# A gated recurrence followed by a soft mixture of experts: the filler transposes of the identity, which the planner puts where TensorE is free in the first chunks, are left out

## The chip, the cores and the metric

The kernel runs on one core of a Trainium2 chip. The metric is device time in microseconds (us) for one execution; lower is better. The core has five engines that this text speaks of: TensorE (PE in the profile, with its weight loads as PEld), VectorE (DVE), ScalarE (ACT), GpSimd (POOL), and SyncE (SP), whose queue issues the DMAs. TensorE runs at one of two clock levels, 1.2 and 2.4 GHz; the profile calls the granted share of the full level PEclk (0.50 and 1.00).

## What is computed

The input is a sequence of 4 x 5056 = 20224 tokens with 256 channels. A gated linear recurrence runs along each sequence, and its result, all tokens in one list, goes through a soft mixture of 8 experts with 4 slots each. Cut to what matters:

```python
a_base = sigmoid(a_param)                       # one number per channel
log_a = 8.0 * sigmoid(r_gate) * log(clip(a_base))
a_t = exp(log_a)
x_gated = sqrt(max(1 - a_t * a_t, 1e-6)) * sigmoid(i_gate) * x
for t in range(S):
    h = a_t[:, t] * h + x_gated[:, t]           # y[:, t] = h
x = y.reshape(B * S, D)                         # 20224 x 256
logits = x @ phi                                # 20224 x 32
d = softmax of logits over the tokens;  c = softmax of logits over the slots
slot_input = d.T @ x                            # 32 x 256
slot_out = relu(slot_input[e] @ w1[e]) @ w2[e]  # for each of 8 experts
out = c @ slot_out
```

## The kernel before

Tokens are taken in quads of 512 (number q), and quads in units p: unit 0 is quad 0 alone, then come units of two quads. Units are grouped in chunks of two, because ScalarE's functions live in different tables and each chunk goes through them once (tanh and exp, sigmoid, square root).

The work on one quad, with the names that the tasks have in the program:

- SP loads r_gate, i_gate and x of the quad (line 553; the first r_gate in two halves, lines 550 and 551) into seven buffers `st` and sixteen buffers `b`.
- TR (line 610): TensorE transposes the 512 x 256 block of r_gate, 8 transposes of 128 x 128, into a PSUM buffer of two banks, of which there are three, `pair_92`, `pair_93` and `pair_94`. At most two of them may be held by TR at a time.
- SR (line 621): ScalarE takes tanh of that block. EX (line 685) turns it into a_t, SQ (line 672, mostly GpSimd) squares it, RT (line 702) takes the square root.
- SI (lines 634 and 636): ScalarE's sigmoid or tanh of i_gate. P1 and U (lines 647 and 656): GpSimd multiplies it by x.
- TU (line 721): TensorE transposes that product into a `pair`, for one half of the channels of one unit: 8 transposes, or 16 where two terms are added.
- ST and SC (lines 738 and 755): VectorE multiplies by the root and runs the scan. SC of one unit continues from SC of the unit before.
- TY (line 779): TensorE transposes the scan's result back, 4 transposes for half a quad, into a single PSUM bank (`one_87` or `one_88`) or a `pair`. YC (lines 793 and 795) copies it to SBUF.

Groups of four quads then feed the logits (line 835), a running maximum (line 848) and the weighted sums over the tokens (line 909). After the last scan come the merge, the experts and the output (lines 1094 to 1390).

What sets the order: no engine chooses at run time. A planner (class `Planner`) plays the work through once, with estimated durations, and writes for each engine one fixed sequence of tasks. ScalarE's sequence of table functions is fixed ahead of that. Where TensorE is free in the plan, no task is ready for it, and the planned time is between `warm_from` (4.0) and `warm_to`, the planner puts in a filler task:

```python
elif e == "PE" and self.warm is not None and (self.warm_from <= now < self.warm_to or self.warm_late(self)):   # 279
    t = self.filler(now)
# filler (307): takes a single bank if more than one is free, else a pair if more than one is free
def e_warm(b):                                                                                                 # 1033
    for _ in range(2):
        nc.tensor.transpose(
            out=t(b)[:, 0, :P] if b.tag == "pair" else t(b)[:, :P], in_=ident, identity=ident)
planner.warm, planner.warm_from, planner.warm_to = e_warm, 4.0, WARMT                                          # 1038
```

A filler task is two transposes of the identity (line 1035). It holds a PSUM buffer from the same lists as the other tasks, nothing reads its result, and it has no input but the constant identity. `warm_late` is never true here, as `LATE` is False.

Of the kernel before, what the change touches and what calls it, by code (L numbers as in the profile page):

```python
# [39 lines left out]
YPM = 2  # L40
XPM = 0
YPQ = 0
WARMT = 60.0
QL = 99
TUP = 15
ACP = -4
# [327 lines left out]
def kernel(  # L374
# [662 lines left out]

    planner.warm, planner.warm_from, planner.warm_to = e_warm, 4.0, WARMT
    planner.pair_max = {"rp": RPM, "up": UPM, "yp": YPM, **dict.fromkeys(("lp", "ep", "ac", "cp"), XPM)}
# [392 lines left out]
```

## Time and profile before

| | |
|---|---|
| median of 3 runs | 305.94 us (305.58 to 306.07) |
| the profiled execution | 304.62 us |
| its span, first to last instruction | 302.8 us |
| its mean granted TensorE clock | 0.995 |
| instructions in the profile | 5814 |
| TensorE busy | 256.7 us, 85% |
| VectorE busy | 251.1 us, 83% |
| ScalarE busy | 250.1 us, 83% |
| GpSimd busy | 207.3 us, 68% |
| DMA | 100.03 MB, mean 330 GB/s |

How to read it: the profile is of one execution, and its 304.62 us hold the span of 302.8 us and 1.8 us around it; the median of the runs is 1.3 us above it. Busy shares are means over the whole span. They differ between the recurrence (to about 210 us), the merge and the experts (to about 245 us) and the output.

### The profile page before, as it was taken

Reading aid. Unit: us, or ns where it says so; the run is one execution under the profiler, and the core shown is the slowest. Engines: PE = TensorE matmul, PEld = TensorE weight load, DVE = VectorE, ACT = ScalarE, POOL = GpSimd, SP = SyncE. Lnnn points to the kernel's source line nnn. Section 1 sums busy time; section 2 is a strip of 40 time slices with the busy share of each in tenths; the row PEclk is TensorE's granted clock in tenths of the full one; section 3 lists DMA queues with packets and bytes.
Section 4 is the critical chain, followed back from the end, with each engine's and each line's share of the span. In section 5 each row is a group of like instructions: output and inputs, shape, how many; then the busy total and the mean of one; then the engine's idle time right before and its main releaser. Section 6 shows DMA issues by size and latency. Waiting matters only on the chain.

```text
span 302.8 us, 5814 instructions
## 1 busy us (share of the span) xinstructions
PE 256.7 (85%) x2181; PEld 191.9 (63%) x2181; DVE 251.1 (83%) x313; ACT 250.1 (83%) x273; POOL 207.3 (68%) x154
## 2 busy tenths in 40 slices
PE   6988759888779989889888988869999999999980
PEld 5977656765555756657566565465545588888760
DVE  0048769999999999899999999989968178999861
ACT  6899999999999999999999999999320058879540
POOL 4383996979969999999997996996216303456200
PEclk9999999999999999999999999999999999999998
DMA  6999899896995978939979889579999419999997
GB/s 249 416 411 409 302 349 333 309 374 260 375 415 206 386 285 295 358 125 360 414 238 374 336 280 411 190 286 393 393 387 388 160 67 391 405 392 407 385 406 288
DMA packets 30433, 100.03 MB, mean 330 GB/s; under 512 B 3395, under 2 KB 3397, under 8 KB 30405
## 3 DMA queue, kind: packets, MB, share of 16 engines
q1 hardware_dynamic: 30400, 99.66, 86.4%
q8 instruction: 17, 0.28, 0.4%
q14 instruction: 12, 0.09, 0.1%
q10 hardware_dynamic: 4, 0.00, 0.0%
HBM read 78.94 MB, written 20.71 MB: 329 GB/s over the span
## 4 chain that ended last, share of the span: by engine, by line
ACT 52%; PE 25%; DVE 9%; issue 7%; DMA 4%; POOL 0%; SPq 0%; DVEq 0%; ACTq 0%
ACT b L702 10%; ACT b L621 10%; ACT b L685 9%; PE bank L1363 8%; ACT st L634 6%; ACT L702 4%; DVE b L755 4%; ACT st L636 3%; ACT L621 3%; ACT L634 3%; PE one L1363 2%; PE bank L1206 2%; DVE pair L738 2%; DMA st<-in_r_gate_dram 2%; PE bank L1340 2%
## 5 line engine op out<-in xcount | busy, mean ns | idle before, releaser
L672 POOL TENSOR_TENSOR b<-b 128x1024 f32<-128x1024 f32 (+1 forms) x40 | 72.0, 1834 | 25.8 <-ACT b L685 23.3
L656 POOL TENSOR_TENSOR b<-st,b 128x1024 f32<-128x1024 f32 (+1 forms) x33 | 76.3, 2339 | 0.2
L738 DVE SCALAR_TENSOR_TENSOR pair<-b,pair 128x1024 f32<-128x1024 f32 (+2 forms) x42 | 48.1, 1155 | 8.9 <-PE pair L721 5.3
L721 PE MATMUL pair<-ident,b 128*128 128x128 f32 x316 | 43.8, 277 | 10.7 <-ACT b L621 5.8
L755 DVE TENSOR_TENSOR_SCAN b<-b,pair 128x1024 f32<-128x1024 f32 (+6 forms) x28 | 52.2, 1883 | 0.2
L610 PE MATMUL pair<-ident,st 128*128 128x128 f32 x316 | 42.6, 281 | 11.5 <-ACT b L621 5.4
L721 PEld LDWEIGHTS pair<-ident,b 128*128 128x128 f32 x316 | 34.5, 141 | 23.6 <-ACT b L621 7.7
L610 PEld LDWEIGHTS pair<-ident,st 128*128 128x128 f32 x316 | 35.0, 143 | 20.6 <-ACT b L621 10.2
L685 ACT ACTIVATE b<-b,ca 128x2048 f32<-128x2048 f32 (+3 forms) x24 | 42.5, 1796 | 0.2
L621 ACT ACTIVATE b<-pair 128x1024 f32<-128x1024 f32 (+1 forms) x40 | 39.9, 1005 | 2.8 <-PE pair L610 2.5
L755 DVE TENSOR_TENSOR_SCAN b<-b,b,pair 128x1024 f32<-128x1024 f32 (+2 forms) x20 | 40.9, 2047 | 0.3
L1363 PE MATMUL bank<-bd,hT 128*128 128x512 f32 x122 | 33.2, 401 | 1.8 <-ACT hT L1351 0.8
L779 PE MATMUL one<-ident,b 128*128 128x128 f32 x224 | 33.0, 278 | 0.6 <-DVE b L755 0.6
L795 DVE COPY yn<-one 128x512 f32<-128x512 f32 x47 | 30.8, 683 | 2.7 <-PE one L779 2.5
L702 ACT ACTIVATE b<-b 128x2048 f32<-128x2048 f32 (+2 forms) x18 | 31.7, 1791 | 0.1
L779 PEld LDWEIGHTS one<-ident,b 128*128 128x128 f32 x224 | 24.9, 141 | 5.6 <-DVE yn L795 2.3
L1306 POOL TENSOR_TENSOR b<-b,rs_all 128x512 f32<-128x512 f32 (+2 forms) x11 | 10.7, 975 | 24.2 <-DVE rs_all L1298 23.2
L1363 PEld LDWEIGHTS bank<-bd,hT 128*128 128x128 f32 x122 | 22.0, 188 | 6.7 <-ACT hT L1351 1.3
L634 ACT ACTIVATE st<-st 128x1024 f32<-128x1024 f32 x26 | 25.9, 1048 | 0.1
L835 PE MATMUL one<-b,phi_sb 128*32 128x512 f32 (+1 forms) x164 | 24.2, 585 | 1.2 <-ACT eS L889 0.7
L1375 ACT COPY st<-bank 128x512 f32<-128x512 f32 x32 | 18.0, 596 | 6.5 <-PE bank L1363 3.8
L1377 DVE COPY st<-bank 128x512 f32<-128x512 f32 x26 | 17.3, 680 | 4.3 <-DMA out_dram<-st 2.9
(143 smaller groups left out, 430.8 us busy)
## 6 DMA issues: line engine op xcount, KB each, us to landing
st<-in_i_gate_dram SPq DMA_DIRECT2D x39, 512.0 KB, 6.2
b<-in_x_dram SPq DMA_DIRECT2D x39, 512.0 KB, 7.0
st<-in_r_gate_dram SPq DMA_DIRECT2D x38, 512.0 KB, 7.3
out_dram<-st SPq DMA_DIRECT2D x35, 512.0 KB, 5.2
b<-in_moe_w_dram SPq DMA_DIRECT2D x26, 512.0 KB, 9.1
st<-in_moe_w_dram SPq DMA_DIRECT2D x6, 512.0 KB, 5.0
out_dram<-st SPq DMA_DIRECT2D x5, 256.0 KB, 2.9
out_dram<-b SPq DMA_DIRECT2D x2, 512.0 KB, 4.4
```

The source lines that it names most:

```text
L610: nc.tensor.transpose(out=o[:, m, :], in_=raw("r", q)[:, m * D + h * P : m * D + (h + 1) * P], identity=ident,)
L621: nc.scalar.activation(dst, t(rp)[:, :, :c], AF.Tanh, scale=0.5)
L634: nc.scalar.activation(v, v, AF.Sigmoid)
L656: eng.tensor_tensor(out=o, in0=a, in1=b, op=ALU.mult)
L672: eng.tensor_tensor(out=t(Nb[p])[:, h, :c], in0=v, in1=v, op=ALU.mult)
L685: nc.scalar.activation(v, v, AF.Exp, scale=ca[:, h : h + 1], bias=ca[:, h : h + 1])
L702: nc.scalar.activation(v, v, AF.Sqrt, bias=quarter if f != 1.0 else f, scale=-f)
L721: nc.tensor.matmul(o[:, m, :], raw(nm, q)[:, m * D + h * P : m * D + (h + 1) * P], ident, is_transpose=True, start=(nm == nms[0] and m == ...
L738: nc.vector.scalar_tensor_tensor(v, t(Nb[p])[:, h, :c], 0.5e-3 if gate_of(quads(p)[0]) == "E" else 1e-3, v, op0=ALU.max, op1=ALU.mult)
L755: nc.vector.tensor_tensor_scan(dst, dst, flat()[:, s0:s1], init, op0=ALU.mult, op1=ALU.add)
L779: nc.tensor.transpose(out=flat()[:, b * D + h * P : b * D + (h + 1) * P], in_=t(A[p])[:, h, o : o + P], identity=ident,)
L1363: nc.tensor.matmul(t(op), t(hT)[:, b * P // 2 : (b + 2) * P // 2], T["bd"][part].rearrange("p i d -> p (i d)"), start=(part == 0), stop=(p ...
```

## The change

One constant is set to zero:

```diff
-WARMT = 60.0
+WARMT = 0.0
```

With `warm_to` at 0.0 the condition on line 279 never holds, and the planner puts in no filler. TensorE's sequence loses the 56 filler tasks, 112 of its 2181 matmuls, and as many weight loads. The other tasks keep their order on ScalarE, VectorE, GpSimd and SP. What else differs is which of the like PSUM buffers a task gets, and one swap on TensorE.

The first place is TensorE's sequence at the start. `st_61`, `st_62` and `st_63` hold r_gate of quads 0, 1 and 2, `st_65` that of quad 3. Before:

```order
L937 MATMUL one_87<-ident,ap_sb 128x2
L610 MATMUL pair_92<-ident,st_61 128x128 x8
L1035 MATMUL one_88<-ident 128x128 x2
L1035 MATMUL pair_93<-ident 128x128 x2
L1035 MATMUL one_87<-ident 128x128 x2
L610 MATMUL pair_94<-ident,st_62 128x128 x8
L1035 MATMUL one_88<-ident 128x128 x2
L1035 MATMUL pair_93<-ident 128x128 x2
L1035 MATMUL one_87<-ident 128x128 x2
L1035 MATMUL pair_92<-ident 128x128 x2
L610 MATMUL pair_93<-ident,st_63 128x128 x8
```

The same place in the changed kernel:

```order
L937 MATMUL one_87<-ident,ap_sb 128x2
L610 MATMUL pair_92<-ident,st_61 128x128 x8
L610 MATMUL pair_93<-ident,st_62 128x128 x8
L610 MATMUL pair_94<-ident,st_63 128x128 x8
L610 MATMUL pair_92<-ident,st_65 128x128 x8
```

The TRs of quads 0 to 3 now follow each other, and the three pairs go round among them.

The second place is TensorE's sequence where the first back transposes (line 779, TY, of `b_68`) stand; `st_66`, `st_61` and `st_62` hold r_gate of the next quads. Before:

```order
L610 MATMUL pair_94<-ident,st_62 128x128 x8
L779 MATMUL one_88<-ident,b_68 128x128 x4
L779 MATMUL one_87<-ident,b_68 128x128 x4
L1035 MATMUL pair_93<-ident 128x128 x2
L1035 MATMUL pair_94<-ident 128x128 x2
L1035 MATMUL pair_93<-ident 128x128 x2
L1035 MATMUL pair_94<-ident 128x128 x2
L1035 MATMUL pair_93<-ident 128x128 x2
L1035 MATMUL pair_94<-ident 128x128 x2
L779 MATMUL one_88<-ident,b_68 128x128 x4
L610 MATMUL pair_93<-ident,st_66 128x128 x8
L779 MATMUL one_87<-ident,b_68 128x128 x4
```

The same place in the changed kernel:

```order
L610 MATMUL pair_94<-ident,st_62 128x128 x8
L779 MATMUL one_88<-ident,b_68 128x128 x4
L779 MATMUL one_87<-ident,b_68 128x128 x4
L779 MATMUL one_88<-ident,b_68 128x128 x4
L779 MATMUL pair_92<-ident,b_68 128x128 x4
L610 MATMUL pair_94<-ident,st_66 128x128 x8
L610 MATMUL pair_93<-ident,st_61 128x128 x8
L779 MATMUL one_87<-ident,b_68 128x128 x4
```

Six fillers are gone, and the fourth TY, now into `pair_92`, stands ahead of the TR of `st_66` where it stood behind it.

The third place is TensorE's sequence around the TUs of the third unit (`b_72`). Before, with eight fillers between its two halves:

```order
L779 MATMUL one_87<-ident,b_68 128x128 x4
L721 MATMUL pair_93<-ident,b_72 128x128 x8
L1035 MATMUL one_88<-ident 128x128 x2
L1035 MATMUL one_87<-ident 128x128 x2
L1035 MATMUL one_88<-ident 128x128 x2
L1035 MATMUL one_87<-ident 128x128 x2
L1035 MATMUL one_88<-ident 128x128 x2
L1035 MATMUL one_87<-ident 128x128 x2
L1035 MATMUL one_88<-ident 128x128 x2
L1035 MATMUL one_87<-ident 128x128 x2
L721 MATMUL pair_92<-ident,b_72 128x128 x8
```

The same place in the changed kernel:

```order
L779 MATMUL one_88<-ident,b_68 128x128 x4
L721 MATMUL pair_94<-ident,b_72 128x128 x8
L721 MATMUL pair_93<-ident,b_72 128x128 x8
L721 MATMUL pair_94<-ident,st_65 128x128 x4
L721 MATMUL pair_94<-ident,b_72 128x128 x4
```

The two TUs of the unit now stand next to each other. From here on both kernels have the same sequence on every engine, and the PSUM buffers of one are those of the other under exchanged numbers.

## Rows read from the trace of the kernel before

**Rows 1.** The page: its head, the busy time of each engine, and the chain of work that ended last, by engine.

```profile
span 302.8 us, 5814 instructions
PE 256.7 (85%) x2181; PEld 191.9 (63%) x2181; DVE 251.1 (83%) x313; ACT 250.1 (83%) x273; POOL 207.3 (68%) x154
ACT 52%; PE 25%; DVE 9%; issue 7%; DMA 4%; POOL 0%; SPq 0%; DVEq 0%; ACTq 0%
```

**Rows 2.** Busy time by stage: from and to, length, then busy us of PE, PEld, DVE, ACT and POOL (with their instructions), granted clock, DMA share, GB/s.

```profile
10.00:45.00 35.00, 27.25 (x234) 25.10 (x233) 20.76 (x18) 34.79 (x30) 26.69 (x13) 1.00 0.97 374
45.00:95.00 50.00, 41.91 (x358) 30.93 (x357) 48.30 (x49) 49.77 (x42) 42.35 (x24) 1.00 0.86 324
95.00:195.00 100.00, 86.30 (x769) 61.28 (x767) 97.91 (x99) 99.56 (x88) 94.23 (x52) 1.00 0.84 312
```

**Rows 3.** ScalarE in order of time: start, us from start to end, operation, count, and in brackets the idle time before it and what ended it.

```profile
5.44 1.02 ACT L621 ACTIVATE b<-pair 128x1024 f32<-128x1024 f32 x1 [1.26 <-PE pair L610]
...
7.46 1.03 ACT L621 ACTIVATE b<-pair 128x1024 f32<-128x1024 f32 x1
9.76 1.03 ACT L621 ACTIVATE b<-pair 128x1024 f32<-128x1024 f32 x1 [1.28 <-PE pair L610]
10.82 2.38 ACT L685 ACTIVATE b<-b,ca 128x1024 f32<-128x1024 f32 x2
...
15.70 1.92 ACT L621 ACTIVATE b<-pair 128x1024 f32<-128x1024 f32 x2
...
34.32 2.01 ACT L634 ACTIVATE st<-st 128x1024 f32<-128x1024 f32 x2
36.23 1.01 ACT L621 ACTIVATE b<-pair 128x1024 f32<-128x1024 f32 x1
...
43.68 1.94 ACT L621 ACTIVATE b<-pair 128x1024 f32<-128x1024 f32 x2
```

**Rows 4.** The fillers: all matmuls of line 1035, by the buffer that they write.

```profile
L1035 PE MATMUL one<-ident 128*128 128x128 f32 x72 | 11.7, 279 | 0.0
L1035 PE MATMUL pair<-ident 128*128 128x128 f32 x40 | 7.3, 283 | 1.8 <-ACT b L621 1.5 <-DVE b L755 0.3
```

**Rows 5.** TensorE in order of time from 3 to 17 us, matmuls and some of the weight loads (PEld) of the fillers.

```profile
3.22 2.18 PE L610 MATMUL pair<-ident,st 128*128 128x128 f32 x8 [0.79 <-DMA st<-in_r_gate_dram]
4.98 0.44 PEld L1035 LDWEIGHTS one<-ident 128*128 128x128 f32 x2
5.41 0.44 PEld L1035 LDWEIGHTS pair<-ident 128*128 128x128 f32 x2
6.38 1.04 PE L610 MATMUL pair<-ident,st 128*128 128x128 f32 x8
7.15 0.25 PEld L1035 LDWEIGHTS one<-ident 128*128 128x128 f32 x2
7.37 0.25 PEld L1035 LDWEIGHTS pair<-ident 128*128 128x128 f32 x2
8.63 1.09 PE L610 MATMUL pair<-ident,st 128*128 128x128 f32 x8 [0.34 <-DMA st<-in_r_gate_dram]
11.53 1.04 PE L610 MATMUL pair<-ident,st 128*128 128x128 f32 x8
```

**Rows 6.** The loads of r_gate of quads 1 and 2 on line 553, issued at 1.64 and 2.07 us: the issues in 2.05 to 2.5 us, and the time from issue to landing (shortest, median, longest of the two).

```profile
L553 SPq DMA_DIRECT2D st<-in_r_gate_dram x2: 424/428/432, 1.6 to 2.1; - x2
DMA to landing us min/median/max: 4.5/5.5/6.5
```

**Rows 7.** TensorE in order of time from 28 to 36 us.

```profile
28.83 1.04 PE L779 MATMUL one<-ident,b 128*128 128x128 f32 x8
30.14 0.44 PE L1035 MATMUL pair<-ident 128*128 128x128 f32 x2 [0.27 <-DVE b L755]
32.11 1.31 PE L1035 MATMUL pair<-ident 128*128 128x128 f32 x10 [1.53 <-ACT b L621]
33.26 0.27 PE L779 MATMUL one<-ident,b 128*128 128x128 f32 x1
34.10 0.55 PE L779 MATMUL one<-ident,b 128*128 128x128 f32 x3 [0.58 <-DVE b L755]
34.49 1.04 PE L610 MATMUL pair<-ident,st 128*128 128x128 f32 x8
```

**Rows 8.** TensorE in order of time from 40 to 46 us, and then rows of VectorE in order of time between 45 and 61 us.

```profile
40.44 0.66 PE L721 MATMUL pair<-ident,b 128*128 128x128 f32 x4 [1.39 <-POOL b L656]
40.94 1.91 PE L1035 MATMUL one<-ident 128*128 128x128 f32 x16
44.75 1.09 PE L721 MATMUL pair<-ident,b 128*128 128x128 f32 x8 [1.91 <-ACT b L621]
...
45.98 1.23 DVE L738 SCALAR_TENSOR_TENSOR pair<-b,pair 128x1024 f32<-128x1024 f32 x1 [1.16 <-PE pair L721]
59.25 1.29 DVE L795 COPY yn<-one 128x512 f32<-128x512 f32 x2 [0.39 <-PE one L779]
```

**Rows 9.** TensorE around its longest gap between two tasks, and its last matmuls.

```profile
196.10 0.60 PE L779 MATMUL one<-ident,b 128*128 128x128 f32 x4
198.87 1.09 PE L779 MATMUL pair<-ident,b 128*128 128x128 f32 x8 [2.17 <-ACT yn L793]
294.22 1.66 PE L1363 MATMUL bank<-bd,hT 128*128 128x512 f32 x6 [0.65 <-DVE hT L1353]
```

**Rows 10.** Busy time by stretch (columns as in rows 2), for the gap and for the end of the span: the granted clock is the third number from the end.

```profile
196.00:199.00 3.00, 0.83 (x8) 0.59 (x7) 2.80 (x2) 2.99 (x4) 3.00 (x2) 1.00 0.80 284
300.00:302.80 2.80, 0.00 (x0) 0.00 (x0) 0.00 (x0) 0.00 (x0) 0.00 (x0) 0.50 0.29 109
```

## The prediction

> **What bounds the kernel now.** I read the page first [rows 1]. TensorE has the largest busy share (85%), but in the chain of work that ended last ScalarE holds 52% and TensorE 25%. Means over the span say little about a change that ends at some 43 us, so the next view is the busy time by stage [rows 2]. From 10 to 195 us ScalarE works for 34.79 + 49.77 + 99.56 = 184.12 of 185 us: it is idle for 0.88 us in all. TensorE, in the stretch with the fillers, is busy for 27.25 of 35 us. So until 195 us the time is set by ScalarE's queue, which runs in a fixed order: what delays one of its instructions delays the rest one for one, as only 0.88 us of idle time can take it up; what makes another engine faster can return those 0.88 us at most.
>
> The third view is ScalarE's own order of time [rows 3]. It waits for TensorE twice, 1.26 us before the SR at 5.44 and 1.28 us before that at 9.76. Both wait for TRs that waited for DMA: the loads of quads 1 and 2 were issued at 1.64 and 2.07 and took 4.5 and 6.5 us, landing at 6.14 and 8.57 [rows 6], and the TR of quad 2 starts at 8.63 [rows 5]. No filler stands in that wait. The places to look at are therefore those at which a TR or a TU ends just before ScalarE or VectorE needs it, and the question there is how fast TensorE runs.
>
> **The fillers themselves.** The change takes away 72 + 40 = 112 matmuls with 11.7 + 7.3 = 19.0 us of busy time [rows 4]. TensorE's busy time should fall by about that, to some 238 us. None of it is on the path by its duration. Fillers that stand ahead of a TR cost that TR something (at 11.53, for instance), but the SR that reads it comes at 15.70 [rows 3, 5], 3.1 us after the TR's end. At 32.11 five fillers wait for ScalarE and stand ahead of the third TY; that TY begins at 33.26, its first transpose runs, and the other three wait until 34.10 for VectorE's scan, whose result they read [rows 7]. Without the fillers they wait for the same scan. So the removal by itself returns 0.0 us; the bounds are 0.0 and -0.88 us (the idle time above), and I take 0.0, since ScalarE's idle time shows no wait for TensorE after 9.76. On SP, VectorE and GpSimd nothing is moved; SP waits for TRs to free `st` buffers, and earlier TRs only let it issue earlier.
>
> **The swap.** The fourth TY now stands ahead of the TR of `st_66`, whose SR is at 36.23. Before, three transposes start at 34.10 and the TR's eight run from 34.49 to 35.53 [rows 7], 0.70 us ahead of the SR [rows 3]. Now 3 + 4 + 8 = 15 transposes lie between the scan's release at 34.10 and the TR's end. At the full clock the weight loads of fillers come two in 0.22 us (7.15 to 7.37), 0.11 us each [rows 5]; eight transposes take 1.09 us [rows 5], so 0.21 us follow the last start. 15 x 0.11 + 0.21 = 1.86, the end is at 35.96, and 0.27 us of cover are left. Cost 0.0 us while the clock is full.
>
> **The clock.** This is the part that the trace of before can't decide. At 4.98 and 5.41 two weight loads take 0.43 us from pair to pair, 0.215 us each; from 7.15 on, 0.11 [rows 5]. TensorE thus starts at its lower level (1.2 GHz) and reaches 2.4 GHz between 5.4 and 6.4 us (the eight transposes at 6.38 take 1.04 us), after having worked almost without a pause since 3.22. From then on the clock stays at 1.00 through every gap; the longest is 2.17 us, from 196.70 to 198.87, and the eight transposes behind it take 1.09 us, full speed [rows 9, 10]. At the end, when the last matmul has ended at 295.88, the granted clock is 0.50 in the stretch from 300 us on [rows 9, 10]. So 2.17 us without work were borne, and some 4 us were not. Eight transposes at the lower level cost 8 x (0.215 - 0.11) = 0.84 us more. Without fillers there are three places:
>
> 1. The TR of quad 2 at 8.63. The TR of quad 0 ends at 5.40, and that of quad 1 can't start before 6.14. If this pause of 0.74 us keeps the clock low past 8.63, the SR at 9.76 is late by up to 0.84 us, and with it all of ScalarE. Bounds 0 and 0.84; I take 0: the clock rose after some 3 us of work from 3.22 on, and two TRs at the lower level, from 3.22 to 5.40 and from 6.14 to about 8, give as much of it before 8.63.
> 2. The TR of `st_66`. From 29.87, where the TYs end, to 34.10 TensorE now has one transpose of 0.27 us to do, where there were six fillers with 0.44 + 1.31 us [rows 7]. The pauses on its two sides are each some 2 us, within the 2.17 that was borne; taken as one stretch of 4.2 us with hardly any work it is like the end of the span. At the lower level the fifteen transposes take 15 x 0.215 + 0.21 = 3.44 us, to 37.54, and the SR, due at 36.23, is late by 1.31 us. Bounds 0 and 1.31; I take 0, by the gap of 2.17, which is the nearer row to two pauses of 2 us.
> 3. The TU at 44.75. From 41.10 to 44.75 TensorE has nothing left to do, 3.65 us, where eight fillers ran for 1.91 [rows 8]. At the lower level these eight transposes end 0.84 us later, and VectorE, which waits for them at 45.98, starts that much later. ScalarE doesn't wait here. VectorE is idle for 50.00 - 48.30 = 1.70 us from 45 to 95 [rows 2], of which 0.98 lie before 45.98; the other 0.72, 0.39 of them at 59.25 [rows 8], take up most. What is left for ScalarE, whose later work reuses the buffers that VectorE frees, is between 0.84 - 0.72 = 0.1 and 0.84 - 0.39 = 0.45 us. With the clock full it is 0; I take 0.1, a small share of the slow case, under what can be told.
>
> Behind 46 us both kernels run the same sequence with the same buffers under other numbers, so that a delay is carried to the end as it is and nothing new arises there.
>
> The Trainium skill (TensorE: Matmul & The Clock Gate, section "HAM oscillation — how this bites in real kernels") says that a TensorE which idles between bursts for long enough falls back to its lower clock, so that each burst begins slowly. The trace agrees at the end of the span and had no such case within it (1.00 behind a gap of 2.17 us). By that rule places 2 and 3 would be slow, and the sum would be 1.31 + 0.1 us instead of about 0.
>
> **The sum.** 0.0 (fillers) + 0.0 (swap) + 0.0 + 0.0 + 0.1 (clock) = about +0.1 us on the profiled execution, 304.62 to 304.7. The median of the runs is 1.32 us above that execution, and the same difference on it gives 305.94 + 0.1 = 306.0 us.
>
> **The rivals.**
>
> - *Slow at the second place.* The clock falls between 29.87 and 34.10, and ScalarE waits 1.31 us at 36.23. It decides from a TR that ends after 36.23, that is, from 3 of the 15 transposes at the lower level on (0.27 / 0.105). For it: 0.27 us of work in 4.2 us, and the lower clock seen at the end of the span. Against it: neither pause alone is longer than the 2.17 us that left the clock full. 305.94 + 1.31 = 307.25 us, with the third place 307.4 to 307.7.
> - *Slow at the start.* The clock rises only after the TR of quad 2: up to 0.84 us, 306.8 us. For it: the rise came after unbroken work that is now broken by 0.74 us. Against it: at the lower level the TRs last twice as long and fill most of the time by themselves. Both together are no sum: a ScalarE that is 0.84 us late has that much more cover at 36.23, and the two give 1.31 us.
> - *Slow at the third place alone.* Up to 0.45 us, 306.4 us.
> - *Faster.* Fillers that wait for `pair` buffers (1.8 us of idle time before them [rows 4]) no longer hold up the tasks behind them, and ScalarE's 0.88 us of idle time go: 305.1 us. Against it: none of this idle time is put down to TensorE.
>
> That the change doesn't do what it says is excluded by the order: all 56 filler tasks are gone, and no other task is added or lost.
>
> **How the numbers follow.** About 0.2% (0.6 us) is what a measurement of this kernel can tell from no change. Chances: the forecast 0.50 (306.0 us), the second place slow 0.29 (307.25 and somewhat above), the start slow 0.09 (306.8, half of it less), the third place alone 0.07 (306.4, within 0.2%), faster 0.05 (305.1). Slower by over 0.2%: 0.29 + 0.08 = 0.37. Faster by over 0.2%: 0.05. The rest, 0.58, is within 0.2%. The range takes in the forecast, with 0.5 us below it for the spread of the runs, and all slow cases up to the second and most of the third place: 305.4 to 307.5. The likeliest case's own range is 305.4 to 306.5.
>
> **What would show it.** Right: TensorE's busy time near 238 us; ScalarE's idle time from 10 to 195 us still under 1 us; the transposes at 34.10 and 44.75 0.11 us apart, the SR at 36.2 without a wait. Slow second place: an idle time of about 1.3 us before the SR near 36 us, put down to TensorE, and weight loads 0.215 us apart behind 34 us. Slow start: an SR that begins after 10 us. Slow third place: VectorE's wait before 46 us longer by 0.8 us. The prediction would be wrong in kind if the time moved by over 0.6 us with ScalarE as full as before, since then something behind 46 us has changed that I hold to be the same.

## The result, and the profile after

The changed kernel takes 309.07 us (median of 19 runs, 306.27 to 311.38). The kernel before, run beside it 19 times, takes 306.07 us (305.10 to 311.23). The ratio, from which runs far above the fastest of their kernel are left out, is 1.0067, interval 1.0040 to 1.0094: 2.05 us on 306.07, against a difference of the medians of 3.00 us. The prediction, 306.0 us with a range to 307.5, was too low.

The profiled execution took 309.64 us, so the two traces stand 5.02 us apart. That is more than the 3.00 us of the medians, as the trace of before, at 304.62 us, lies below all 19 runs of it here. The page after, its head, busy times, the granted clock in 40 slices of 7.7 us (in tenths), and the chain that ended last:

```profile
span 307.9 us, 5594 instructions
PE 255.8 (83%) x2069; PEld 189.1 (61%) x2069; DVE 251.5 (82%) x313; ACT 251.0 (82%) x273; POOL 208.4 (68%) x154
PEclk9965995999999999999999999979999999999998
ACT 41%; PE 26%; DVE 15%; DMA 9%; issue 6%; SPq 1%; POOL 0%; DVEq 0%; ACTq 0%
```

The 112 matmuls are gone and had taken 19.0 us [rows 4], yet TensorE's busy time fell by 0.9 us only [rows 1]; the prediction had it near 238 us. Part of the 19.0 us overlapped with other matmuls: at 0.11 us from start to start the 112 come to some 112 x 0.11 = 12 us (an estimate), so the remaining transposes give some 11 us back by taking longer. The clock row shows where: third, fourth and seventh slice, and the 27th (200 to 208 us). The same in windows (columns as in rows 2):

```profile
10.00:45.00 35.00, 22.47 (x143) 20.21 (x141) 18.54 (x18) 32.86 (x28) 25.40 (x13) 0.80 0.89 342
45.00:95.00 50.00, 41.18 (x330) 31.69 (x331) 46.86 (x46) 49.59 (x42) 41.28 (x23) 0.93 0.90 344
95.00:195.00 100.00, 87.92 (x760) 61.67 (x760) 98.26 (x101) 99.53 (x87) 94.24 (x52) 1.00 0.83 309
7.00:11.00 4.00, 3.31 (x16) 3.27 (x16) 0.69 (x1) 1.57 (x2) 0.00 (x0) 1.00 1.02 406
20.00:25.00 5.00, 3.65 (x16) 3.28 (x16) 1.89 (x4) 4.97 (x5) 4.92 (x2) 0.50 1.03 410
33.00:45.00 12.00, 7.31 (x61) 6.41 (x59) 8.99 (x11) 10.90 (x9) 11.35 (x7) 1.00 0.68 243
47.00:52.00 5.00, 4.15 (x20) 4.15 (x21) 2.23 (x3) 4.97 (x4) 1.33 (x2) 0.50 1.03 416
203.00:206.00 3.00, 3.00 (x16) 3.00 (x15) 1.98 (x3) 2.79 (x3) 3.00 (x3) 0.50 0.85 244
```

One reading of the granted clock misleads: the traces have no record of it ahead of its first rise (at 11.6 us here), and the views print that time as 1.00, as from 7 to 11 us, where the transposes below are 0.215 us apart. A mean clock leaves the slow start out as well.

ScalarE, idle for 0.88 us from 10 to 195 us before [rows 2], is now idle for 35.00 - 32.86 + 50.00 - 49.59 + 100.00 - 99.53 = 3.02 us, 2.14 of them in the first window. Its waits, in order of time (columns as in rows 3):

```profile
9.69 1.02 ACT L621 ACTIVATE b<-pair 128x1024 f32<-128x1024 f32 x1 [2.15 <-PE pair L610]
11.40 1.02 ACT L621 ACTIVATE b<-pair 128x1024 f32<-128x1024 f32 x1 [0.68 <-PE pair L610]
...
33.58 1.03 ACT L621 ACTIVATE b<-pair 128x1024 f32<-128x1024 f32 x1 [0.82 <-PE pair L610]
...
39.32 1.03 ACT L621 ACTIVATE b<-pair 128x1024 f32<-128x1024 f32 x1 [0.46 <-PE pair L610]
```

The SR that began at 9.76 [rows 3] begins at 11.40, and two SRs that had not waited do so, at 33.58 and at 39.32 (36.23 before). TensorE, in order of time:

```profile
7.69 3.67 PE L610 MATMUL pair<-ident,st 128*128 128x128 f32 x16 [2.05 <-DMA st<-in_r_gate_dram]
11.55 1.08 PE L610 MATMUL pair<-ident,st 128*128 128x128 f32 x8 [0.19 <-DMA st<-in_r_gate_dram]
14.12 1.06 PE L610 MATMUL pair<-ident,st 128*128 128x128 f32 x8 [1.49 <-DMA st<-in_r_gate_dram]
16.68 1.06 PE L610 MATMUL pair<-ident,st 128*128 128x128 f32 x8 [1.50 <-DMA st<-in_r_gate_dram]
20.53 1.94 PE L721 MATMUL pair<-ident,b 128*128 128x128 f32 x8 [2.79 <-DVE b L656]
22.27 1.91 PE L610 MATMUL pair<-ident,st 128*128 128x128 f32 x8
...
37.43 0.55 PE L779 MATMUL one<-ident,b 128*128 128x128 f32 x3 [1.92 <-DVE b L755]
37.81 0.60 PE L779 MATMUL pair<-ident,b 128*128 128x128 f32 x4
38.25 1.91 PE L610 MATMUL pair<-ident,st 128*128 128x128 f32 x16
...
47.85 1.97 PE L721 MATMUL pair<-ident,b 128*128 128x128 f32 x8 [4.46 <-ACT b L621]
...
202.26 1.55 PE L779 MATMUL pair<-ident,b 128*128 128x128 f32 x8 [2.17 <-ACT yn L793]
203.60 1.06 PE L779 MATMUL one<-ident,b 128*128 128x128 f32 x4
```

Eight transposes take 1.04 to 1.09 us at the full clock and 1.9 to 2.2 at the lower level [rows 5]. So the 16 from 7.69 on run low (16 x 0.215 + 0.21 = 3.65). The clock then rises, is full for three TRs with pauses of 1.49 and 1.50 us between them, and is low again for the eight transposes behind the pause of 2.79 us and for those that follow. At the second place of the prediction the clock is full (1.00 from 33 to 45 us): the fourth TY, which the swap puts ahead of the TR of `st_66`, stands at 37.81, and the SR of `st_66` begins 39.32 - 37.43 = 1.89 us behind the start of the three TYs. At the third place the clock is low behind a pause of 4.46 us. Near 200 us the gap that left the clock full before [rows 9] is the same 2.17 us; behind it the transposes slow down.

To place the loss I compare the start of the same instruction in two traces, as here of a ScalarE table load in the kernel before and in the changed one:

```profile
189.45 1.28 ACT L634 ACT_TABLE_LOAD   x1
```

```profile
192.83 1.28 ACT L634 ACT_TABLE_LOAD   x1
```

They are 192.83 - 189.45 = 3.38 us apart. The table has this for five table loads of ScalarE (named by their time in the profiled execution of before), for the merge's first matmul (line 1111, 226.74) and for the span's end, in every trace of the study; the last column is the stretches, in us of that trace, in which the clock was low between its first rise and the last 10 us of the trace, where it falls in all of them. The traces with an e were taken on four chips (e1 to e4; e5, e8, e9, e10; e11 to e14; e15 to e18).

| trace | us | 19.49 | 33.03 | 42.38 | 61.81 | 189.45 | 226.74 | span | clock low |
|---|---|---|---|---|---|---|---|---|---|
| before | 304.62 | 0 | 0 | 0 | 0 | 0 | 0 | 0 | none |
| after | 309.64 | 1.62 | 2.54 | 3.10 | 3.39 | 3.38 | 5.05 | 5.02 | 18-32, 46-53, 203-206 |
| e18_after_2 | 311.36 | 2.02 | 2.00 | 5.10 | 5.11 | 5.12 | 6.79 | 6.75 | 20-30, 37-44, 51-54, 204-208 |
| e1_no_filler | 309.89 | 1.49 | 2.38 | 2.55 | 2.55 | 3.66 | 5.31 | 5.27 | 18-32, 39-42, 69-73, 203-206 |
| e2_start_only | 308.32 | 0.10 | 0.09 | 2.14 | 2.15 | 2.17 | 3.71 | 3.71 | 17-28, 34-41, 48-52, 202-205 |
| e3_up_to_24 | 307.78 | 0.84 | 0.82 | 0.81 | 0.82 | 0.85 | 2.50 | 3.16 | 36-39, 46-50, 200-203 |
| e4_all_but_start | 306.69 | 1.35 | 1.35 | 1.34 | 1.34 | 1.38 | 1.39 | 2.04 | none |
| e5_from_30 | 308.19 | 1.74 | 1.72 | 2.28 | 2.28 | 2.30 | 3.66 | 3.57 | 15-25, 35-38, 202-206 |
| e12_only_200 | 307.67 | 2.01 | 2.87 | 3.06 | 3.06 | 3.06 | 3.08 | 3.04 | 19-32, 39-43 |
| e8_gap_200 | 305.48 | 0.94 | 0.94 | 0.92 | 0.93 | 0.93 | 0.95 | 0.86 | 46-50 |
| e9_early | 304.97 | 0.44 | 0.42 | 0.42 | 0.42 | 0.41 | 0.43 | 0.35 | 46-49 |
| e14_double_tr | 307.97 | 2.57 | 2.79 | 3.42 | 3.41 | 3.41 | 3.42 | 3.34 | 24-27 |
| e13_four | 311.21 | 5.14 | 5.21 | 6.57 | 6.57 | 6.55 | 6.56 | 6.59 | none |
| e11_best | 306.80 | 0.67 | 0.65 | 2.20 | 2.19 | 2.19 | 2.21 | 2.18 | 33-37 |
| e10_before_again | 305.38 | 0.23 | 0.21 | 0.80 | 0.79 | 0.77 | 0.78 | 0.76 | 34-38 |
| e15_before_2 | 309.32 | 2.91 | 2.89 | 3.31 | 3.32 | 3.32 | 4.69 | 4.71 | 36-39, 49-53, 203-206 |
| e16_before_3 | 305.94 | 1.34 | 1.32 | 1.32 | 1.33 | 1.31 | 1.32 | 1.31 | 46-50 |
| e17_before_4 | 304.70 | 0.09 | 0.08 | 0.08 | 0.08 | 0.05 | 0.07 | 0.08 | none |

After against before: 1.62 us at the start, 2.54 - 1.62 = 0.92 to 33 us, 0.56 to 42, 0.29 to 62, nothing to 189, 1.67 in the stretch with the gap near 200 us, nothing to the end. A delay of ScalarE is carried as it is: at 61.81 and at 189.45 the columns agree within 0.04 us in all traces but one (e1, whose clock fell at 69).

### The profile page after: what moved, and what is told of

Same layout as the page of the kernel before. It is cut to its first block, busy times and chain, and to the rows that moved or that the text cites. A ratio compares the mean times of both kernels' runs of the same rounds, so it can differ in the third digit from the quotient of the medians.

```text
span 307.9 us, 5594 instructions
## 1 busy us (share of the span) xinstructions
PE 255.8 (83%) x2069; PEld 189.1 (61%) x2069; DVE 251.5 (82%) x313; ACT 251.0 (82%) x273; POOL 208.4 (68%) x154
## 4 chain that ended last, share of the span: by engine, by line
ACT 41%; PE 26%; DVE 15%; DMA 9%; issue 6%; SPq 1%; POOL 0%; DVEq 0%; ACTq 0%
ACT b L621 9%; ACT b L685 8%; ACT b L702 7%; DVE b L755 6%; DMA st<-in_r_gate_dram 5%; PE bank L1363 5%; ACT st L634 4%; PE pair L721 4%; DMA out_dram<-st 4%; ACT st L636 3%; DVE pair L738 3%; ACT L702 3%; PE pair L610 3%; PE bank L1206 2%; ACT L621 2%
## 5 line engine op out<-in xcount | busy, mean ns | idle before, releaser
L721 PE MATMUL pair<-ident,b 128*128 128x128 f32 x316 | 48.3, 297 | 14.6 <-ACT b L621 7.3
L721 PEld LDWEIGHTS pair<-ident,b 128*128 128x128 f32 x316 | 38.8, 153 | 27.7 <-ACT b L621 9.0
L610 PE MATMUL pair<-ident,st 128*128 128x128 f32 x316 | 45.3, 292 | 11.6 <-DMA st<-in_r_gate_dram 7.9
L610 PEld LDWEIGHTS pair<-ident,st 128*128 128x128 f32 x316 | 37.2, 149 | 21.4 <-ACT b L621 8.4
L835 PE MATMUL one<-b,phi_sb 128*32 128x512 f32 (+1 forms) x164 | 25.8, 585 | 1.1 <-ACT eS L889 0.7
L779 PE MATMUL pair<-ident,b 128*128 128x128 f32 x96 | 15.0, 287 | 6.6 <-DVE b L755 3.5
```

The source lines that it names most:

```text
L610: nc.tensor.transpose(out=o[:, m, :], in_=raw("r", q)[:, m * D + h * P : m * D + (h + 1) * P], identity=ident,)
L721: nc.tensor.matmul(o[:, m, :], raw(nm, q)[:, m * D + h * P : m * D + (h + 1) * P], ident, is_transpose=True, start=(nm == nms[0] and m == ...
L779: nc.tensor.transpose(out=flat()[:, b * D + h * P : b * D + (h + 1) * P], in_=t(A[p])[:, h, o : o + P], identity=ident,)
```

## The experiments

**Theory.** The fillers kept the clock full; without them it falls in TensorE's pauses, and what ScalarE then waits for comes late. **First rival.** It is the swap and the other PSUM buffers. **Second rival.** The first loads land later in these runs, and the rest is chance.

All edits are to the kernel before. In the first five, the planner still places all 56 filler tasks, so that order and buffers stay as they were, and those outside KEEP do nothing.

**e1_no_filler.** All 56 do nothing.

```diff
-WARMT = 60.0
+WARMT = 60.0; KEEP = ()
-        for _ in range(2):
+        for _ in range(2 if next(fillers) in KEEP else 0):
```

(`fillers = iter(range(9999))` stands on line 1038 from here on.)

> The planner still plans the 56 fillers, so that every task keeps the order and the PSUM buffers of the kernel before, but none of them is emitted. Clock theory (the time is lost because TensorE falls to its lower level without the fillers): like the changed kernel, ratio 1.005 to 1.010, granted clock 0.50 in stretches before 55 us. Order theory (the swapped TY and the other buffers cost the time): ratio 1.000, and the SRs near 31 and 36 us as early as before.

308.76 us (307.24 to 310.15, 12 runs); the kernel before beside it 307.97 (305.19 to 310.47, 35 runs, shared by e1 to e4); ratio 1.0033, interval 0.9995 to 1.0071. The runs alone don't settle it: the ratio lies below the expected 1.005 to 1.010, and its interval holds 1. Its trace has three of the four waits of ScalarE in the changed kernel, none at 38.77, and the low clock (columns as above; then TensorE):

```profile
9.56 1.02 ACT L621 ACTIVATE b<-pair 128x1024 f32<-128x1024 f32 x1 [2.07 <-PE pair L610]
11.27 1.02 ACT L621 ACTIVATE b<-pair 128x1024 f32<-128x1024 f32 x1 [0.68 <-PE pair L610]
...
33.42 1.03 ACT L621 ACTIVATE b<-pair 128x1024 f32<-128x1024 f32 x1 [0.80 <-PE pair L610]
...
38.77 1.02 ACT L621 ACTIVATE b<-pair 128x1024 f32<-128x1024 f32 x1
```

```profile
20.00:30.00 10.00, 7.71 (x35) 7.38 (x36) 4.12 (x6) 9.91 (x9) 5.03 (x3) 0.50 1.03 410
```

```profile
37.31 0.55 PE L779 MATMUL one<-ident,b 128*128 128x128 f32 x3 [1.92 <-DVE b L755]
37.70 1.04 PE L610 MATMUL pair<-ident,st 128*128 128x128 f32 x8
```

With the order of before and no filler it loses 5.27 us of span where the change loses 5.02. The first rival falls as the main cause. It is not nothing: without the swap the SR of `st_66` begins 38.77 - 37.31 = 1.46 us behind the start of the three TYs, in the changed kernel 1.89, also at the full clock. The four transposes between, 4 x 0.11 = 0.44 us, are the difference. From 33 to 42 us e1 loses 0.17 and e12, which has no swap either, 0.19, where the change loses 0.56.

**e2_start_only, e3_up_to_24, e4_all_but_start.** The same with `KEEP = range(0, 7)`, `range(0, 42)` and `range(7, 56)`: the first seven fillers alone (to some 12 us), the first 42, all but the first seven.

> As the first, but the first 7 fillers (before 8.4 us in the kernel before) are emitted. Clock theory: the SR at 9.76 is on time again, some 1 us of the loss is gone, the clock falls later as in the changed kernel; ratio 1.002 to 1.007. Order theory: 1.000. If the start is all that costs: 1.000 too, but then the third run of this call is no better than this one.

308.25 us (307.25 to 310.95, 12 runs), 1.0039, interval 1.0001 to 1.0078. The start costs 0.10 us in place of 1.62, but that these seven fillers hold that place isn't shown: the load of quad 1 took 4.5 us to land here, as in the trace of before, and 6.0 in the changed kernel. Then the clock falls at 17 us and again at 34, and the SR of `st_66` is 2 us late; ScalarE, and the window around it:

```profile
38.36 1.03 ACT L621 ACTIVATE b<-pair 128x1024 f32<-128x1024 f32 x1 [1.94 <-PE pair L610]
```

```profile
36.00:41.00 5.00, 5.00 (x25) 5.00 (x24) 1.62 (x3) 3.03 (x4) 5.00 (x3) 0.50 0.33 111
```

> As the first, but the first 42 fillers (up to 23.3 us) are emitted; those at 30 to 33 and at 41 to 43 us are not. Clock theory: granted clock 1.00 up to 30 us at least; what is left is the loss of a low clock behind the pauses before 34 and before 45 us, 0 to 1.7 us, ratio 1.000 to 1.006. Order theory: 1.000.

308.44 us (305.87 to 310.44, 12 runs), 1.0031, interval 0.9988 to 1.0074. After 0.84 us at the start nothing more is lost up to 189 us. Then the gap near 200 us costs 2.50 - 0.85 = 1.65; TensorE there:

```profile
199.73 1.97 PE L779 MATMUL pair<-ident,b 128*128 128x128 f32 x8 [2.17 <-ACT yn L793]
```

Eight transposes in 1.97 us, where before had 1.09 behind the same gap [rows 9].

> As the first, but all fillers except the first 7 are emitted. Clock theory: the TRs of quads 1 and 2 run at the lower level, the SR at 9.76 is 0.8 to 1.6 us late and this stays to the end, ratio 1.003 to 1.005; the clock is 1.00 from 12 us on. Order theory: 1.000.

307.41 us (306.59 to 308.93, 12 runs), 0.9988, interval 0.9955 to 1.0021, not told apart from before and below the expected 1.003 to 1.005: the first seven fillers aren't missed in the runs. Those behind them are: e1, on the same chip and with the same order, lies 308.76 - 307.41 = 1.35 us higher by the medians of 12 runs each (0.2 to 2.8 us by resampling them, an estimate). In its trace e4 loses 1.35 us at the start and nothing between there and 227 us, with a full clock from its rise at 10.6 us on. The start is that of the changed kernel, 16 transposes in a row at, first, the lower level:

```profile
7.77 3.30 PE L610 MATMUL pair<-ident,st 128*128 128x128 f32 x16 [2.16 <-DMA st<-in_r_gate_dram]
```

**e5_from_30.** `KEEP = range(42, 56)`, the last 14.

> Order and buffers of the kernel before; only the last 14 fillers (at 30 to 33 and 41 to 43 us in the kernel before) are emitted. Clock theory: the start is late by some 1 us as without fillers, the clock falls in 15 to 30 us as in the run without fillers, and is full again behind 34 and behind 44 us; ratio 1.001 to 1.004. If the two late pauses were the main cost, this run would be near the kernel before (1.000); if the stretch from 15 to 30 us is, near the run without fillers (1.003).

307.85 us (305.97 to 308.82, 12 runs); before beside it 307.23 (304.47 to 310.66, 29 runs, shared by e5, e8 and e9); 1.0045, interval 1.0010 to 1.0080. Start 1.74 us, 0.56 from 33 to 42 us, and 1.36 near 200, although fillers ran at 32 to 35 and at 43 to 45 us.

The stretch from 10 to 30 us divides all 18 traces. The six without fillers there (after, e18, e1, e2, e5, e12) have a fall between 14 and 20 us; of the twelve with fillers there, only e14, whose TRs are doubled, has one before 30 us. That it is the fillers that hold the clock there is thus shown.

**e8_gap_200.** All fillers stay, and one more of 16 transposes is placed in the pause ahead of the gap near 200 us.

```diff
-WARMT = 60.0
+WARMT = 210.0
-        for _ in range(2):
+        for _ in range(2 if next(fillers) < 56 else 16):
```

> The kernel before with one more filler of 16 transposes in TensorE's gap of 2.17 us near 197 us. The clock fell behind this gap in the traces of the changed kernel and of three of its variants, and held in that of the kernel before. Clock theory: the clock is 1.00 from 195 to 210 us, and the runs of the kernel before that are 2 to 4 us above its fastest become rarer; ratio 0.993 to 0.999. If the gap only happens to lie there, the runs scatter as before: ratio 1.000.

305.54 us (304.69 to 308.18, 12 runs), 0.9989, interval 0.9956 to 1.0022. The pause of 2.17 us is down to 0.42 and the clock holds; TensorE, then two windows:

```profile
196.12 1.97 PE L1035 MATMUL pair<-ident 128*128 128x128 f32 x16 [0.73 <-ACT b L621]
...
199.82 1.09 PE L779 MATMUL pair<-ident,b 128*128 128x128 f32 x8 [0.42 <-ACT yn L793]
```

```profile
47.00:49.00 2.00, 2.00 (x12) 2.00 (x11) 1.60 (x2) 2.00 (x2) 0.20 (x1) 0.50 1.03 420
195.00:210.00 15.00, 13.26 (x132) 9.85 (x124) 14.46 (x14) 14.89 (x19) 13.63 (x10) 1.00 0.92 329
```

The median is not told apart from that of before. The clock fell at 46 us, at the third place of the prediction; ScalarE lost 0.01 us by it (0.92 to 0.93 in the table).

**e12_only_200.** That filler alone: `range(16 if next(fillers) > 55 else 0)`, WARMT 210.

> No filler in the first 60 us, and one of 16 transposes in the gap of 2.17 us near 200 us. Clock theory: the first 80 us as in the run without fillers (ScalarE 2 to 3.7 us late by then), and nothing more is lost from 195 us on, where that run lost 0.9 us to 208 us and 0.8 us more to the end; ratio 1.5 us better than without fillers, 1.000 to 1.004. If the loss near 200 us only follows from being late: no better than without fillers.

307.59 us (305.40 to 313.53, 12 runs); before beside it 306.78 (304.53 to 311.45, 24 runs, shared by e11 to e14); 1.0031, interval 0.9996 to 1.0066. The window has the full clock, and from 189 us to the merge 0.02 us are lost, where the six traces without that filler and without the full set (e4 apart) lose 1.4 to 1.7:

```profile
195.00:210.00 15.00, 13.17 (x146) 9.95 (x143) 14.38 (x14) 14.92 (x19) 14.44 (x10) 1.00 0.78 286
```

The 3.06 us lost before 62 us remain. The saving is read from the trace alone: the ratio, 1.0031, is no better than the 1.0033 of e1 (on another chip), where 1.5 us had been expected.

**e9_early.** Fillers also ahead of the first TR, none in the next seven places, and one near 200 us. In the planner `warm_from` is 1.5, WARMT 210, and

```diff
-        for _ in range(2):
+        for _ in range((0, 2, 16)[(n := next(fillers)) not in range(4, 11) and 1 + (n > 67)]):
```

> As the run with the filler near 197 us, and four fillers more ahead of the first TR, from about 1.5 us on. Clock theory: the clock rises before the TR of quad 2 in every run, that TR takes 1.1 us and the SR that reads it begins within 1.2 us of the landing; the slowest starts go and the ratio is 0.990 to 0.998. If the start's scatter comes from the loads alone: as the run with the filler near 197 us.

305.12 us (304.36 to 307.52, 12 runs), 0.9977, interval 0.9945 to 1.0008. The interval holds 1. The clock is full from 5.0 us on, ahead of the TR of quad 1, and the start costs 0.44 us although its load landed late; TensorE:

```profile
7.55 1.09 PE L610 MATMUL pair<-ident,st 128*128 128x128 f32 x8 [1.51 <-DMA st<-in_r_gate_dram]
...
9.13 1.04 PE L610 MATMUL pair<-ident,st 128*128 128x128 f32 x8
```

**e13_four.** Fillers of four transposes: `range(4 if next(fillers) < 56 else 16)`, WARMT 210.

> Fillers of 4 transposes where the kernel before has 2, and the one of 16 near 197 us. Clock theory: the clock is 1.00 from its first rise to the last matmul, if the fillers fill what is left of the pauses; the loads' TRs that stand behind longer fillers are up to 0.4 us later, with cover; ratio 0.990 to 0.999, like the run with the filler near 197 us. If longer fillers stand in the way: slower than that run by 0.3 us or more.

311.29 us (310.53 to 311.93, 6 runs), 1.0163, interval 1.0121 to 1.0205: a miss, with the highest ratio of all, at a clock that was full from 9.1 us on. TensorE:

```profile
9.41 0.60 PE L1035 MATMUL one<-ident 128*128 128x128 f32 x4
...
11.16 1.04 PE L610 MATMUL pair<-ident,st 128*128 128x128 f32 x8
```

Four fillers lie between the two TRs, 11.16 - 9.41 = 1.75 us, and nine more, up to 15.96, ahead of the next. A TR whose load has landed waits here until the fillers ahead of it are done.

**e14_double_tr.** What does a delay at the start cost? The transposes of quads 1 and 2 run twice, with the same result.

```diff
-                for m in range(n):
+                for m in list(range(n)) * (2 if q in (1, 2) else 1):
```

> The kernel before, but the TRs of quads 1 and 2 make each of their 8 transposes twice (the same result twice), so that they last as long at the full clock as at the lower one, 16 x 0.11 + 0.21 = 2.0 us instead of 1.1. If it is the length of the TR of quad 2 that delays the rest, ScalarE is 0.9 us later than with single TRs from 19 us on and stays so to 195 us, and the best runs are near 306.1 us. If ScalarE's queue has cover that I overlook, less than 0.3 us is left by 195 us.

309.64 us (307.97 to 310.53, 4 runs), 1.0101, interval 1.0050 to 1.0152. The delay was larger than expected, 2.57 us: the load of quad 1 landed late, and both doubled TRs and the four fillers between them lay on the path. TensorE, then ScalarE:

```profile
7.71 1.97 PE L610 MATMUL pair<-ident,st 128*128 128x128 f32 x16 [0.86 <-DMA st<-in_r_gate_dram]
...
10.39 1.91 PE L610 MATMUL pair<-ident,st 128*128 128x128 f32 x16
```

```profile
12.34 1.03 ACT L621 ACTIVATE b<-pair 128x1024 f32<-128x1024 f32 x1 [1.59 <-PE pair L610]
```

3.41 us at 62 us become 3.34 us of span. The clock held behind the gap near 200 us.

**e11_best.** As e9, with four transposes in each filler from the 56th on and 16 near 200 us.

```diff
-        for _ in range(2):
+        for _ in range(0 if (n := next(fillers)) in range(4, 11) else 16 if n > 67 else 4 if n > 54 else 2):
```

> Four fillers ahead of the first TR, the one of 16 transposes near 197 us, and 4 transposes in each filler from 31 us on, where two traces had a granted clock of 0.50 from 46 to 50 us. Clock theory: clock 1.00 from 5.2 us to the last matmul; that stretch cost ScalarE nothing in those two traces, so the median is that of the run with early fillers, 305.1, within 0.3 us.

305.21 us (303.74 to 309.28, 12 runs), 0.9960, interval 0.9930 to 0.9989: 0.4% below the kernel before beside it. Its one traced run (306.80 us) still shows a low clock at 33 us, and fillers in the way of the SR at 38.41:

```profile
32.77 4.29 PE L1035 MATMUL pair<-ident 128*128 128x128 f32 x22 [1.52 <-ACT b L621]
```

**e10_before_again, e15_before_2, e16_before_3, e17_before_4.** The kernel before, unedited, to see how it scatters.

> The kernel before once more, for a second trace of it: its runs scatter from 305.2 to 310.5 us. Clock theory: if this run is above 307 us, its trace has stretches with a granted clock of 0.50, near 200 us or in the first 60 us; if it is near 305.5 us it has none. If the scatter has another cause: slow without such a stretch.

> The kernel before again, for its trace. If the fall near 200 us comes by chance in both kernels: about two in five such runs are above 307 us, and exactly these have a granted clock of 0.50 between 195 and 210 us and a merge (line 1111) that begins 1.5 us or more later than ScalarE's delay at 195 us accounts for. If it belongs to the change: never here, and slow runs have another cause.

> As the run before it: the same kernel, the same two readings.

> As the run before it: the same kernel, the same two readings.

305.38, 309.32, 305.94 and 304.70 us. In e10 the clock fell at 34 us, where none had been expected of so quick a run, and cost 0.59 (0.21 to 0.80 in the table). In e15 the clock rose only at 12 us, so that fillers at the lower level stood ahead of a TR (start 2.91 us), and it fell near 200 us (1.37). TensorE in e15:

```profile
9.58 0.63 PE L1035 MATMUL one<-ident 128*128 128x128 f32 x2
...
11.28 1.36 PE L610 MATMUL pair<-ident,st 128*128 128x128 f32 x8
...
202.21 1.19 PE L779 MATMUL pair<-ident,b 128*128 128x128 f32 x8 [2.17 <-ACT yn L793]
```

So the kernel before has the changed kernel's loss too, less often. Its 93 runs beside and among the experiments order by mean granted clock: at 0.99 or more 37 runs, median 305.62 us; from 0.98 to 0.99 48 runs, 308.28; below that 8 runs, 309.59. The 19 runs of the changed kernel are all between 0.951 and 0.969.

**e18_after_2.** The changed kernel once more.

> The changed kernel again, for its trace. Both readings: a granted clock of 0.50 in 15 to 32 us, and ScalarE 2 to 3.7 us late at 102 us. If the fall near 200 us comes by chance, it can hold here; if it belongs to the change, it falls here too.

311.36 us. Start 2.02, nothing from there to 33 us, then the second place at more than its predicted size, with the clock low from 37 to 44 us; ScalarE:

```profile
41.33 1.02 ACT L621 ACTIVATE b<-pair 128x1024 f32<-128x1024 f32 x1 [3.00 <-PE pair L610]
```

5.10 - 2.00 = 3.10 us from 33 to 42, and 1.67 near 200. ScalarE was 5.1 us late at 62 us, more than expected.

## Why the prediction was wrong

The frame held: ScalarE's order sets the time, and a delay of it is carried one for one (e14, and from 62 to 189 us all rows of the table but e1's). The term for the clock failed, which was taken as 0.0 + 0.0 + 0.1, and with it the term for the swap, taken as 0.0. The term for the fillers themselves, 0.0, is not measured apart; fillers ahead of a TR did cost in e13 and e15.

*"2.17 us without work were borne."* This was the step on which the first two zeros hung, and it failed. One gap in one trace was read as a bound. The same gap of 2.17 us near 200 us was followed by a full clock in six of the traces and by a low one in seven; and the clock fell at 18.4 us, behind three TRs at full speed with pauses of 1.49 and 1.50 us between them and some 0.7 us into the third pause. The Trainium skill (TensorE: Matmul & The Clock Gate, section "A second HAM failure mode: psum-queue depth-cycling") tells of a kernel whose TensorE pauses shortly and often between groups of matmuls and swings between its levels. The trace agrees in the stretch from 11.55 to 20.53, with its pauses of 1.49 and 1.50 us. The rule on idling between bursts, which the prediction took from the Trainium skill and set aside, would have made the second and third places slow, 307.35 us in all, still short. The trace of the changed kernel agrees with it at the third place alone (0.50 behind a pause of 4.46 us); at the second it shows 1.00.

*First place, 0 with a bound of 0.84.* Measured 1.62 and 2.02 in the changed kernel, 1.35 to 2.01 in the four traces of e1, e4, e5 and e12 that lack the first fillers. The bound was mis-sized, since it counted the TR of quad 2 alone. The TR of quad 1 began at 6.38 in the trace of before, the earliest of 18 traces; in the others it begins between 6.89 and 8.08, in most of them because its load lands later. Then both TRs lie in a row on the path, and the lower level costs 16 x (0.215 - 0.11) = 1.68 us. So this loss comes of a late load and a low clock together: e9 had the TR of quad 1 at 7.55 with a full clock and lost 0.44. How much of it belongs to the change is open, as the second rival isn't excluded here. From issue to landing that load took 5.9 to 6.4 us in the six traces without the first seven fillers and 4.5 to 6.2 in the eight that have them as before; and the two of these whose load was as late, e15 (6.1) and e16 (6.2), lost 2.91 and 1.34 us with the fillers in place.

*A place not named.* Between 18 and 32 us TensorE runs low and the SR at 33.58 waits 0.82: 0.92 us in the table, 0.89 in e1 and 0.86 in e12. In e18, e2 and e5 the clock fell there too but was full again by 30 us, and nothing was lost. The prediction looked only at the pauses near 8, 30 and 41 us.

*Second place and swap, 0 with a bound of 1.31.* In the trace of the changed kernel the clock was full here, and the cost from 33 to 42 us, 0.56, is for the most part the swap. The prediction's 15 transposes took their 1.86 us (37.43 to 39.29), but its cover of 0.27 us was gone: VectorE's scan released them at 37.43, 3.33 us later than before, when ScalarE was 2.54 us late. The scan was late in e1 as well (37.31, with the clock low from 18 to 32 us), but without the swap the SR didn't wait. In e18 and e2 the clock did fall here, and the cost is 3.10 and 2.05 us. There the rival "slow at the second place" was the right mechanism and too small.

*Third place, 0.1.* The size was near: 0.29 us in the changed kernel, within the 0.1 to 0.45 of the slow case, and 0.01 in e18 and e8. The clock, taken as full there, fell to 0.50 in all three.

*"Nothing new arises" behind 46 us.* Wrong by the largest single term: 1.67 us near 200 us. That it is the clock is shown by the traces of e8 and e12, which fill the gap and lose 0.02. Why the fall belongs to the change is open. Of the traces without the filler at 200 us, all six that lack part of the fillers from 4 to 60 us, e4 apart, fall there; of the seven others (five of before, e4, e14) only e15 does. TensorE's program is the same in both from 60 us on, and the shift doesn't decide: with 3.41 us (e14) the clock held, with 3.38 it fell, with 0.77 (e10) held, with 0.85 (e3) fell.

*The base.* Three runs, 305.58 to 306.07, were taken for the spread of the kernel; it goes from 304.47 to 311.45. The kernel before stands on the same edge, which e15 shows.

So the step that failed is the zero for the clock, read from one gap in one trace. What the runs showed in its place is falls of the clock that cost ScalarE 0.92 us behind 18 us and 1.67 near 200, with some 0.4 us for the swap between them. Also open: 0.65 us that e3 and e4 lose behind 227 us.

## What to carry to other kernels

Where the engine that sets the time waits on small bursts of TensorE, fillers can pay by holding the clock, if they are short and not ahead of work that is due: here two transposes each helped, and four cost 1.6%. A gap that left the clock full in one trace bounds nothing, so count runs and take several traces before a clock term is set to zero. Look for the loss wherever the same gap recurs, however far behind the edit.

## What the runs showed of the hardware that had not been expected

The same pause, 2.17 us after the same instructions, was followed by either clock level from run to run of one program (e15 against e10, e16 and e17). The clock fell with TensorE busy for 2.76 of 6.00 us at the full level just before:

```profile
12.00:18.00 6.00, 2.76 (x22) 2.11 (x20) 1.49 (x1) 5.97 (x7) 4.15 (x3) 1.00 1.03 413
```

And a kernel at a mean clock of 0.99 had the highest ratio of the study (e13): a full clock is no gain where the fillers that hold it stand in the way.
